# Keeping the first sequence's spectral mixing on chip, with its filters fetched into both partition halves

## The chip, the cores and the metric

The kernel runs on one core of one Trainium2 chip. The metric is device microseconds (us) of one execution, lower is better. "Fast" below means that a run lies within 1.5% of the fastest of its kernel.

PE is TensorE (matrix products), DVE VectorE, ACT ScalarE, POOL GpSimd, and SP SyncE, which only issues transfers here. The transfers that one of them issues are its queue. A matrix product leaves its result in a bank of PSUM (the `ps` tiles of the kernel); copying it out is an eviction. The granted clock is the share of PE's full clock that it was allowed. An item's lag is how much later its Silu instruction starts than that of the same item in the kernel before.

## The reference, cut to what matters

The lines are merged and shortened; they compute the same.

```python
def _attn_ref(x, filt_r, filt_i):              # x: 8 x 3008 x 256, filters: 1505 x 256
    X = np.fft.rfft(x, axis=1)
    return np.fft.irfft(X * (filt_r + 1j * filt_i)[None], n=x.shape[1], axis=1)

def _moe_ref(x, w_gate, w_val, w_out, rms_g):  # 24064 tokens, d_model 256, d_ff 1536
    xn = x / np.sqrt(np.mean(x * x, axis=-1, keepdims=True) + 1e-06) * rms_g
    g = xn @ w_gate
    return (g / (1.0 + np.exp(-g)) * (xn @ w_val)) @ w_out
```

Each of the 8 sequences is mixed along time by a filter in the frequency domain ("mixing"). Every token then passes through a normalization and a gated feed-forward network (FFN).

## The kernel before

The transform of length 3008 = 47 x 64 is made of matrix multiplications. Step A transforms over 64, B over 47, then comes the product with the filters, then B and A backward. Between A and B, and between the two backward steps, the data must change their layout. The kernel does that by writing to DRAM and reading back: `z` between A and B, `g` behind B backward.

The FFN is 8 x 6 x 12 = 576 items of the same work. Mixing of sequence b+1 runs between the items of sequence b, so it is mostly hidden. Mixing of sequence 0 has nothing to hide behind: it is **the opening**, the time before the first gate matmul (`pg`).

The filters are fetched by POOL's queue, chunk by chunk (8 of the 32 frequency columns each), into the lower half of the partitions, in transfers of 24, 16 and 7 rows. On-chip copies make the upper half, with the sign of the imaginary filter turned:

```python
def f_load(c):
    for src, dst in ((filt_r, fr), (filt_i, fi)):
        t = dst[c]
        nc.gpsimd.dma_start(t[0:24, :, :].rearrange("p a d -> p (a d)"),
                            raw(src, c * KC, [[64 * D, 24], [1, KC * D]]))
        lo = 1 if c == 0 else 0
        for a, e in ((0, 16), (16, 23)):
            nc.gpsimd.dma_start(t[32 + a:32 + e, lo:KC, :],
                                raw(src, 64 * (a + 1) - c * KC - lo,
                                    [[64 * D, e - a], [-D, KC - lo], [1, D]]))
        ...
def f_dup(c):
    nc.vector.tensor_copy(out=fr[c][HALF:P], in_=fr[c][0:HALF])
    nc.scalar.activation(out=fi[c][HALF:P], in_=fi[c][0:HALF], func=AXT.Copy, scale=-1.0)
...                                   # the opening, cut
for c in range(NC):
    for i in range(3):
        a_unit(0, 3 * c + i)          # A
    z_store(0, c)                     # to DRAM
for c in range(3):
    t2_load(0, c)                     # and back
gate(st[0]["t2"][0][0:1, 0, 0:1])     # POOL waits for the first reload ...
f_load(1); f_load(2)                  # ... before it issues more filters
f_dup(0)
for i in range(19):
    if i < 16:
        b_unit(0, i)                  # B and the products with the filters (DVE, POOL)
    ...                               # f_load(3), f_dup(1..3), FFN weights
    if i >= 3:
        bi_unit(0, i - 3)             # B backward
        if i % 2 == 0:
            g_store(0, i // 2 - 2)    # to DRAM
for c in range(NXC):
    t4_load(0, c)                     # and back
norm_first()                          # A backward, normalization
```

Of the kernel before, what the change touches and what calls it, by code (L numbers as in the profile page):

```python
# [10 lines left out]
FP32 = mybir.dt.float32  # L11
# [24 lines left out]
KC = 8  # L36


def _make_tables():
# [21 lines left out]
    for k2 in range(K2):  # L61
        for s in range(48):

            if s < 24:
                k = k2 + 64 * s
                sign, q = 1.0, s
            else:
                j = s - 23
                k = 64 * j - (k2 if k2 else 32)
                sign, q = -1.0, 32 + s - 24  # L70
                if j == 24 and k2:
                    continue
# [25 lines left out]
    wi0 = wi[:, 0] * S_INV_B  # L98
    return wa.astype(f), (wai * S_INV_A).astype(f), wb.astype(f), wi0.astype(f), np.eye(P).astype(f)
# [3 lines left out]
def kernel(  # L103
# [13 lines left out]
    wa_np, wai_np, wb_np, wi0_np, id_np = _make_tables()  # L117
    wa_d = nc.inline_tensor(wa_np, name="wa_t").ap()
    wai_d = nc.inline_tensor(wai_np, name="wai_t").ap()
    wb_d = nc.inline_tensor(wb_np, name="wb_t").ap()  # L120
    wi0_d = nc.inline_tensor(wi0_np, name="wi0_t").ap()
    id_d = nc.inline_tensor(id_np, name="id_t").ap()
# [8 lines left out]
    t1p = ctx.enter_context(tc.tile_pool(name="t1p", bufs=2))  # L131
    t2p = ctx.enter_context(tc.tile_pool(name="t2p", bufs=3))
    sp = ctx.enter_context(tc.tile_pool(name="sp", bufs=3))
    ssp = ctx.enter_context(tc.tile_pool(name="ssp", bufs=3))
# [4 lines left out]
    rp = ctx.enter_context(tc.tile_pool(name="rp", bufs=2))  # L139
# [3 lines left out]
    op = ctx.enter_context(tc.tile_pool(name="op", bufs=2))  # L143
# [7 lines left out]
    wai = glob.tile([P, P], FP16)  # L151
    ident = glob.tile([P, P], FP16)
    wb = glob.tile([KR, K2, P], FP16)
    wi = glob.tile([P, K2, 2, P], FP16)
    fr = [glob.tile([P, KC, D], FP32, name="fr%d" % c) for c in range(K2 // KC)]
    fi = [glob.tile([P, KC, D], FP32, name="fi%d" % c) for c in range(K2 // KC)]
# [24 lines left out]
    def bank(i, name):  # L181

        pool, tag = ((psM, "mx"), (psG, "pg"), (psV, "pv"), (psB, "mb"))[i]
        return pool.tile([P, 512], FP32, tag=tag, name=name)

    def a_unit(b, i):
        c, r = divmod(i, XC // 2)
        if r == 0:

            st[b]["t1"][c] = (t1p.tile([P, XC, D], FP16, tag="t1", name="t1") if b else  # L190
                              t4p.tile([P, XC, D], FP16, tag="t4", name="t1"))
        ps = bank(0 if b else i % 3, "psa")
        dst = st[b]["t1"][c][:, 2 * r:2 * r + 2, :]
        nc.tensor.matmul(ps, wa, st[b]["x"][c][:, 2 * r:2 * r + 2, :], start=True, stop=True)  # L194
        src = ps.rearrange("p (a d) -> p a d", a=2)
        nc.scalar.activation(out=dst, in_=src, func=AXT.Copy)  # L196
# [13 lines left out]

    def b_unit(b, i):
        ps = bank(3 if b else (0, 1, 3)[i % 3], "psb").rearrange("p (a d) -> p a d", a=2)
        for u in range(2):
            k = 2 * i + u
            nc.tensor.matmul(ps[:, u, :], wb[:, k, :], st[b]["t2"][k // KC][:, k % KC, :],  # L215
                             start=True, stop=True)
        c, r = divmod(2 * i, KC)
        f1, f2 = fr[c][:, r:r + 2, :], fi[c][:, r:r + 2, :]
        if b:
            s1 = sp.tile([P, 2, D], FP16, tag="s1", name="s1")  # L220
            s2 = sp.tile([P, 2, D], FP16, tag="s2", name="s2")
# [8 lines left out]
        if (b == 0 and i % 2 and i > 4) or (b == 1 and i % 3 == 1):  # L230
            eng = nc.gpsimd
            v = yp.tile([P, 2, 512], FP32, tag="y", name="v")
            v = v[:, 0, :].rearrange("p (a d) -> p a d", a=2)
            nc.scalar.activation(out=v, in_=ps, func=AXT.Copy)
            ps = v
# [3 lines left out]

    def swap_unit(b, i, h):  # L240
# [3 lines left out]
        if h:  # L244
            s = ssp.tile([P, 2, D], FP16, tag="s", name="s")
# [3 lines left out]
    def bi_unit(b, i):  # L249
        ss = st[b]["s"].pop(i)  # L250
        ps = bank(0 if b else 2, "psi").rearrange("p (a d) -> p a d", a=2)
        n = len(ss)
        for u in range(2):
            for q in range(n):
                nc.tensor.matmul(ps[:, u, :], wi[:, 2 * i + u, q, :], ss[q][:, u, :],  # L255
# [10 lines left out]
    def t4_load(b, c):  # L266
        t = t4p.tile([P, XC, D], FP16, tag="t4", name="t4")
        w = XC - 1 if c == NXC - 1 else XC
        for h in range(2):
            for ri in range(2):  # L270
# [3 lines left out]
                (nc.scalar if b == 0 and c == 0 and h else nc.sync).dma_start(  # L274
                    t[p0:p0 + 32, 0:wh, :], g_d[b, :, r0:r0 + wh, :])
# [7 lines left out]
    def n_unit(b, m, dh):  # L283
# [5 lines left out]
        for q in range(nq(b, m)):  # L289
            n1p = 4 * m + q  # L290
            nc.tensor.matmul(ps[:, ts(q, P)],  # L291
                             st[b]["t4"][n1p // XC][:, n1p % XC, ds(dh * P, P)], wai,
# [32 lines left out]
    def rho_load(b, m):  # L325
        rb = rp.tile([P, 4 * P], FP32, tag="rb", name="rb")
# [4 lines left out]
    def norm_first():  # L331
# [3 lines left out]
        for dh in range(2):  # L335
            ps = bank(1 + dh, "psn")
            for q in range(4):
                nc.tensor.matmul(ps[:, ts(q, P)], st[0]["t4"][q // XC][:, q % XC, ds(dh * P, P)], wai,
# [6 lines left out]
        q_unit(0, 0)  # L345
        scale_split(0)
        scale_apply(0, 1)
# [35 lines left out]
    po_of = {}  # L383

# [15 lines left out]
    def down(b, m, jt):  # L400
# [11 lines left out]
        if jt == JT - 1:  # L412
            o3 = op.tile([P, 4, D], FP32, tag="o3", name="o3")
# [22 lines left out]
    def f_load(c):  # L436
        for src, dst in ((filt_r, fr), (filt_i, fi)):
            t = dst[c]
            nc.gpsimd.dma_start(t[0:24, :, :].rearrange("p a d -> p (a d)"),
                                raw(src, c * KC, [[64 * D, 24], [1, KC * D]]))  # L440
            lo = 1 if c == 0 else 0
            for a, e in ((0, 16), (16, 23)):
                nc.gpsimd.dma_start(t[32 + a:32 + e, lo:KC, :],
                                    raw(src, 64 * (a + 1) - c * KC - lo,
                                        [[64 * D, e - a], [-D, KC - lo], [1, D]]))
            if c == 0:
                nc.gpsimd.dma_start(t[32:56, 0, :], raw(src, 32, [[64 * D, 24], [1, D]]))

    def f_dup(c):
        nc.vector.tensor_copy(out=fr[c][HALF:P], in_=fr[c][0:HALF])  # L450
        nc.scalar.activation(out=fi[c][HALF:P], in_=fi[c][0:HALF], func=AXT.Copy, scale=-1.0)

    def wi_group(g):

        ps = bank(1 + g % 2, "pst").rearrange("p (a d) -> p a d", a=4)
        lo = 1 if g == 0 else 0
        for a in range(lo, 4):
            nc.tensor.matmul(ps[:, a, :], wb[:, 4 * g + a, :], ident[0:KR, :], start=True, stop=True)
        k = slice(4 * g + lo, 4 * g + 4)
        nc.scalar.activation(out=wi[:, k, 0, :], in_=ps[:, lo:4, :], func=AXT.Copy, scale=S_INV_B)  # L460
        for p0 in (0, HALF):
            nc.vector.tensor_scalar(out=wi[p0:p0 + HALF, k, 1, :],
                                    in0=ps[HALF - p0:P - p0, lo:4, :], scalar1=S_INV_B,
                                    scalar2=None, op0=ALU.mult)
# [13 lines left out]
    def wb_load(c):  # L478
        nc.sync.dma_start(wb[:, c * KC:(c + 1) * KC, :], wb_d[:, c * KC:(c + 1) * KC, :])

    with tc.manual_schedule():
# [5 lines left out]
        nc.sync.dma_start(wa, wa_d)  # L487
        nc.sync.dma_start(ident, id_d)
        wb_load(0)
        wb_load(1)  # L490

        for c in range(NC):
            for t in (fr[c], fi[c]):
                if c < 2 or (c == 2 and t is fr[c]):
                    nc.vector.memset(t[0:HALF], 0.0)
                else:
                    nc.scalar.activation(out=t[0:HALF].rearrange("p a d -> p (a d)"),
                                         in_=mhalf[0:HALF, 0:1].to_broadcast([HALF, KC * D]),
                                         func=AXT.Copy, scale=0.0)
        nc.vector.memset(ones, 1.0)  # L500
        f_load(0)
        for c in range(NC):
            for i in range(3):
                a_unit(0, 3 * c + i)
            z_store(0, c)
            if c == 1:
                wb_load(2)
                wb_load(3)
                wi_group(0)
                wi_group(1)  # L510
        for c in range(3):
            t2_load(0, c)
        gate(st[0]["t2"][0][0:1, 0, 0:1])
        f_load(1)
        f_load(2)
        nc.sync.dma_start(wi[:, 0], wi0_d)
        nc.sync.dma_start(wai, wai_d)
        with nc.allow_non_contiguous_dma(reason="one gain a partition"):
            nc.sync.dma_start(gsb, moe_rms_g.rearrange("(a p) -> p a", p=P))
        for g in range(2, 8):  # L520
            wi_group(g)
        f_dup(0)
        for i in range(19):
            if i < 16:
                b_unit(0, i)
            if i == 5:
                t2_load(0, 3)
                f_load(3)
            if i == 9:
                w_load(0)  # L530
            if i % 4 == 2 and i // 4 + 1 < NC:
                f_dup(i // 4 + 1)
            if i >= 3:
                bi_unit(0, i - 3)
                if i % 2 == 0:
                    g_store(0, i // 2 - 2)
        for c in range(NXC):
            t4_load(0, c)
        gate(st[0]["t4"][0][0:1, 0, 0:1])
        norm_first()  # L540
        w_load(1)
        w_load(2)
        for dh in range(2):
            n_unit(0, 1, dh)
            sq_unit(0, 1, dh)
        for c in range(NXC):
# [25 lines left out]
        for b in range(1, B):  # L572
# [19 lines left out]
            for i in range(16):  # L592
# [5 lines left out]
                at(s0 + lag, bi_unit, b, i)  # L598
                if i % 2 == 1:
# [54 lines left out]
```

## Time and profile before

The median is 968.98 us of 3 runs (965.85 to 969.09). The profiled execution has a span of 965.5 us.

| what | value | view |
|---|---|---|
| TensorE (PE) busy from 300 to 900 us | 596.87 of 600 us, clock 1.00 | table of stretches |
| first gate matmul | 84.48 us | timeline |
| z round trip: last eight stores issued, first B matmul | 18.9 to 22.5, 28.41 us | timeline |
| g round trip: last eviction, end of reload | 71.09, 76.20 us | chain of waits |

The page cuts the span into 40 slices of 24 us. Each digit is a busy share, or the granted clock, in tenths.

```profile
PE   3345978898999999999999999999999999999997
PEclk8566999999999999999999999999999999999999
DMA  8869774764357345753457535742354322422211
```

PE is starved in the first four slices and nearly full from the eleventh on. Only the opening has much to give. The next lines are from the table of stretches of the kernel before. The columns are the stretch, its length, busy time and instruction count of PE, PE weight loads, DVE, ACT and POOL, then the granted clock, the mean busy share of the 16 DMA engines, and GB/s.

```profile
15.00:20.00 5.00, 0.54 (x7) 0.24 (x4) 2.86 (x5) 1.94 (x4) 0.00 (x0) 0.61 0.93 261
35.00:41.00 6.00, 0.93 (x5) 0.48 (x4) 3.06 (x4) 0.00 (x0) 2.91 (x4) 0.50 0.82 108
300.00:900.00 600.00, 596.87 (x4187) 375.12 (x4185) 458.10 (x722) 420.31 (x717) 237.81 (x178) 1.00 0.46 103
```

From 15 to 20 us (mostly tables and z) the DMA engines moved 261 GB/s at share 0.93. From 35 to 41 us (filters alone) they moved 108 GB/s at share 0.82.

This is the chain of waits of the kernel before (start, duration, what):

```profile
28.43 0.61 POOL gate L469
...
30.66 8.87 DMA fi<-in_filt_i_dram
...
39.81 6.26 DMA fi<-in_filt_i_dram
...
50.57 6.67 DMA fi<-in_filt_i_dram
...
71.11 2.27 DMA g_tmp<-t
...
73.58 2.63 DMA t<-g_tmp
```

Two round trips stand in the chain (`gate` waits for the z reload, then `g_tmp`), and three waits for filters lie between them.

### The profile page before, as it was taken

To read this page: it belongs to the slowest core of one execution; us is meant where nothing else is said; L and a number is where in the kernel's file an instruction comes from. 1 tells how busy PE (TensorE), PEld (TensorE's weight loads), DVE (VectorE), ACT (ScalarE), POOL (GpSimd) and SP (SyncE) were. 2 spreads that over 40 slices of the span, in tenths; PEclk is the share of its full clock that TensorE was granted. 3 is DMA by queue.
4 is the path that set the end of the run, shared out by engine and by line. 5 is a ranking of instruction groups with operands and counts; after the bars stand their busy time and mean duration, and the time that the engine had idled before them with its cause. 6 is when DMAs were issued, how large, how long until landed. Compare 5 with 4: busy or idle time off the path is not lost.

```text
span 965.5 us, 17242 instructions
## 1 busy us (share of the span) xinstructions
PE 880.0 (91%) x6031; PEld 547.8 (57%) x6031; DVE 668.1 (69%) x1039; ACT 630.1 (65%) x1066; POOL 373.1 (39%) x325
## 2 busy tenths in 40 slices
PE   3345978898999999999999999999999999999997
PEld 1223545565655666666666666566666666666654
DVE  6633445577777788687877878688868888555554
ACT  7343667576766776577766776587756776576543
POOL 3474335325551455226542445135522554033200
PEclk8566999999999999999999999999999999999999
DMA  8869774764357345753457535742354322422211
GB/s 196 141 119 174 158 166 108 149 165 91 87 110 171 81 87 110 162 137 95 94 119 159 114 89 90 171 101 72 100 116 112 89 61 58 117 62 53 47 34 44
DMA packets 95542, 106.45 MB, mean 110 GB/s; under 512 B 17304, under 2 KB 70680, under 8 KB 95264
## 3 DMA queue, kind: packets, MB, share of 16 engines
q1 hardware_dynamic: 85808, 87.39, 38.1%
q0 software_dynamic: 9552, 17.77, 12.1%
q8 instruction: 47, 0.77, 0.3%
q14 instruction: 39, 0.32, 0.1%
q10 hardware_dynamic: 96, 0.20, 0.1%
HBM read 70.09 MB, written 49.90 MB: 124 GB/s over the span
## 4 chain that ended last, share of the span: by engine, by line
PE 70%; DMA 10%; issue 6%; DVE 6%; POOL 4%; ACT 3%; SPq 1%; POOLq 0%; DVEq 0%; ACTq 0%
PE po L409 21%; PE pg L392 21%; PE pv L392 20%; DVE hh L397 3%; PE psi L255 3%; DMA fi<-in_filt_i_dram 2%; DMA rb<-r_tmp 2%; PE psb L215 2%; PE psn L291 2%; PE psa L194 2%; DVE o L415 1%; DMA t<-g_tmp 1%; POOL s L246 1%; DMA z_tmp<-t 1%; DMA g_tmp<-t 1%
## 5 line engine op out<-in xcount | busy, mean ns | idle before, releaser
L397 DVE TENSOR_TENSOR hh<-pv,sg 128x512 f16<-128x512 f32 (+1 forms) x576 | 391.6, 680 | 231.4 <-ACT sg L396 114.3
L396 ACT ACTIVATE sg<-pg 128x512 f16<-128x512 f32 (+1 forms) x576 | 338.8, 588 | 241.6 <-PE pg L392 232.7
L409 PE MATMUL po<-wo,hh 128*128 128x256 f16 x2256 | 343.2, 272 | 2.7 <-DVE o L415 1.3
L392 PE MATMUL pg<-xn,wg 128*128 128x512 f16 (+1 forms) x1152 | 338.4, 375 | 0.0
L392 PE MATMUL pv<-xn,wv 128*128 128x512 f16 (+1 forms) x1152 | 338.3, 375 | 0.0
L409 PEld LDWEIGHTS <-hh 128*128 128x128 f16 x2256 | 216.2, 98 | 112.7 <-issue 13.1
L246 POOL TENSOR_TENSOR s<-s,s 128x512 f16<-128x512 f16 x96 | 110.6, 1152 | 359.9 <-DVE s L243 290.4
L392 PEld LDWEIGHTS <-wv 128*128 128x128 f16 x1152 | 112.7, 98 | 131.6 <-issue 1.1
L377 POOL TENSOR_TENSOR xn<-y,rb 128x1024 f16<-128x1024 f32 (+1 forms) x46 | 128.8, 2800 | 59.2 <-DMA rb<-r_tmp 52.1
L243 DVE TENSOR_TENSOR s<-psb,fi 64x512 f16<-64x512 f32 x192 | 132.1, 688 | 5.9
L392 PEld LDWEIGHTS <-wg 128*128 128x128 f16 x1152 | 109.1, 98 | 13.8 <-issue 1.8
L260 ACT ACTIVATE t<-psi 96x512 f16<-96x512 f32 x128 | 75.4, 592 | 29.0 <-PE psi L255 16.5
L296 ACT ACTIVATE y<-psn,gsb 128x512 f32<-128x512 f32 (+1 forms) x94 | 63.7, 678 | 12.5 <-PE psn L291 4.8
L317 POOL TENSOR_TENSOR rho<-u,mhalf 128x4 f32<-128x4 f32 (+1 forms) x48 | 48.4, 1009 | 56.5 <-DVE u L315 56.1
L255 PEld LDWEIGHTS <-wi 128*128 128x128 f16 x320 | 32.6, 103 | 65.1 <-issue 29.0
L223 DVE TENSOR_TENSOR s<-psb,fr 128x512 f16<-128x512 f32 x96 | 65.5, 682 | 4.7 <-PE psb L215 4.2
L196 ACT ACTIVATE t<-psa 128x512 f16<-128x512 f32 x96 | 56.4, 602 | 12.6 <-PE psa L194 6.6
L215 PE MATMUL psb<-t,wb 96*128 96x256 f16 x256 | 51.6, 286 | 9.4 <-DMA t<-z_tmp 8.8
L255 PE MATMUL psi<-s,wi 128*128 128x256 f16 x256 | 46.2, 272 | 9.9 <-POOL s L246 5.7
L302 ACT ACTIVATE sq<-psn 128x512 f16<-128x512 f32 (+1 forms) x94 | 54.8, 582 | 0.0
L194 PE MATMUL psa<-xc,wa 128*128 128x512 f16 x96 | 36.9, 398 | 16.7 <-DMA xc<-in_x_dram 9.2
L291 PEld LDWEIGHTS <-t 128*128 128x128 f16 x368 | 28.7, 99 | 21.9 <-issue 1.2
(58 smaller groups left out, 382.4 us busy)
## 6 DMA issues: line engine op xcount, KB each, us to landing
out_dram<-o SPq DMA_DIRECT2D x84, 256.0 KB, 3.3
z_tmp<-t SPq DMA_DIRECT2D x128, 96.0 KB, 2.4
t<-z_tmp SPq DMA_DIRECT2D x32, 384.0 KB, 5.1
g_tmp<-t SPq DMA_DIRECT2D x64, 192.0 KB, 3.4
xc<-in_x_dram POOLq DMA_DIRECT2D x56, 192.0 KB, 6.0
rb<-r_tmp SPq DMA_DIRECT2D x42, 256.0 KB, 4.4
t<-g_tmp SPq DMA_DIRECT2D x102, 96.0 KB, 3.1
out_dram<-o SPq DMA_DIRECT2D x12, 192.0 KB, 3.0
```

Of the source, the lines that this page charges most:

```text
L215: nc.tensor.matmul(ps[:, u, :], wb[:, k, :], st[b]["t2"][k // KC][:, k % KC, :], start=True, stop=True)
L223: nc.vector.tensor_tensor(out=s1, in0=ps, in1=f1, op=ALU.mult)
L243: nc.vector.tensor_tensor(out=s2[a], in0=ps[e], in1=f2[e], op=ALU.mult)
L246: nc.gpsimd.tensor_tensor(out=s, in0=s1, in1=s2, op=ALU.add)
L255: nc.tensor.matmul(ps[:, u, :], wi[:, 2 * i + u, q, :], ss[q][:, u, :], start=(q == 0), stop=(q == n - 1))
L260: nc.scalar.activation(out=st[b]["t3"][c][:, 2 * r:2 * r + 2, :], in_=ps[0:KR], func=AXT.Copy)
L296: nc.scalar.activation(out=y[:, dh, 0:w], in_=ps[:, 0:w], func=AXT.Identity, scale=gsb[:, dh:dh + 1])
L377: nc.gpsimd.tensor_tensor(out=xv, in0=yv, in1=rv.unsqueeze(1).to_broadcast([P, 2, n, P]), op=ALU.mult)
L392: nc.tensor.matmul(ps[:, 0:w], wt[:, dt_, ts(jt, P)], xn[:, dt_, 0:w], start=(dt_ == 0), stop=(dt_ == 1))
L396: nc.scalar.activation(out=sg[:, 0:w], in_=pg[:, 0:w], func=AXT.Silu)
L397: nc.vector.tensor_tensor(out=hh[:, 0:w], in0=pv[:, 0:w], in1=sg[:, 0:w], op=ALU.mult)
L409: nc.tensor.matmul(po[s4 // 2][:, s4 % 2, :], hh[:, ts(s4, P)], wo[:, jt, :], start=(jt == 0 and s4 % 2 == 0), stop=(jt == JT - 1 and (s4 ...
```

## The change

Its intent: sequence 0 no longer goes through DRAM. A and B backward are computed with operands swapped, so that channels lie on the partitions, and 16-bit transposes on PE change the layout. Filters are fetched straight into both halves of the partitions (chunk 0 is still copied), so no copies are needed. The imaginary filter arrives with the same sign in both halves; sequence 0 is served by a table `ws` with turned signs. Sequences 2 and later need the sign in the upper half, and four POOL passes (`negate`) turn it while sequence 1 is mixed.

```diff
-    def f_load(c):
+    def f_load(c, p0, part):
+        n, k0 = FC[c], (0, 8, 16)[c]                  # chunks of 8, 8 and 16 columns
...
+            if part == 0:
+                nc.sync.dma_start(t[p0:p0 + 24, :, :].rearrange("p a d -> p (a d)"),
+                                  raw(src, k0, [[64 * D, 24], [1, n * D]]))
...
+            a, e = ((0, 16), (16, 23))[part - 1]
+            eng = nc.gpsimd if (part == 2 and c) else nc.sync
+            eng.dma_start(t[p0 + 24 + a:p0 + 24 + e, lo:n, :],
+                          raw(src, 64 * (a + 1) - k0 - lo, [[64 * D, e - a], [-D, n - lo], [1, D]]))
...
+    def negate(c, r, n):
+        t = fi[c][HALF:P, r:r + n, :]
+        nc.gpsimd.tensor_scalar(out=t, in0=t, scalar1=-1.0, scalar2=None, op0=ALU.mult)
+    def at_unit(m, dh): ...      # A: x is the stationary operand, channels on partitions
+    def t1_unit(g): ...          # 8 transposes with a strided source, 1 or 2 evictions
+    def bit_unit(i): ...         # B backward: 8 matmuls of 96 columns per unit
+    def t2_unit(j, eng): ...     # 4 transposes, one eviction
...
-            z_store(0, c)
-            t2_load(0, c)
-                    g_store(0, i // 2 - 2)
-            t4_load(0, c)
+        for part in range(3):
+            for p0 in (0, HALF):
+                f_load(1, p0, part)
...                               # chunk 2 likewise
+        for i in range(16 + LAG):
+            if i < 16:
+                b_unit(0, i)
+            if i % 2 == 0 and i // 2 + 2 < 8:
+                t1_unit(i // 2 + 2)
+            if i >= LAG:
+                bit_unit(i - LAG)
...
+                if b == 1 and i in (3, 7, 11, 15):
+                    at(s0 + 2, negate, min(i // 4, 2), 8 if i == 15 else 0, 8)
```

## The prediction

The 200 GB/s stands as an estimate, between the measured 108 (filters alone) and 261 GB/s (tables and z). The sum: 3.9 of some 9 MB by 20 us, the rest at 200 GB/s gives the last filters at 42 to 46 us, eight DVE units of 1.38 us from 42 us on end at 53 to 54, and with 13 us behind them the first gate matmul comes near 66 us, 18 us earlier. The 13 us, and the "1 or 2 us" for sign flips and reload, are estimates too. The "cold" 0.13 us was measured at a granted clock of 0.50 (the kernel before, 77 to 78 us).

> **What bounds the kernel now.** The table of stretches shows two regimes. Between 300 and 900 us TensorE is the limit (99% busy, clock 1.00). Up to 85 us it starves: mostly below half busy, at granted clock 0.5 for much of the time after 15 us. The timeline puts the first gate matmul at 84.4 us. Nearly all of the change's worth is how much earlier that matmul starts.
>
> The chain of waits in the opening is made of transfers: x until about 14 us; the z store and reload (last store issued at 18.9, first B matmul at 28.4 us); then filters, issued one behind another by POOL (waits of 8.9, 6.3 and 6.7 us on fi), with halves copied by DVE and ACT (1.2 to 2.1 us each); then g store and reload (70.5 to 77.0 us). From the first normalization matmul to the first gate matmul are 7.4 us.
>
> **Removed.** z round trip: about 10 us. g round trip: about 6.5 us. Three of four pairs of filter copies, most weight-table copies on DVE, POOL's serial issue of filters.
>
> **Added.** 112 transposes, and 128 narrow matmuls instead of 64 wide ones. Cold 128x128 pairs of load and matmul take about 0.13 us (8 in 1.03 us at 77 us), so 112 transposes are about 15 us of TensorE time, mostly hidden behind filter transfers. All final transposed tiles are queued before the first gate matmul: I estimate 13 us from the last mixing eviction to that matmul, where 7.4 us were needed after the reload. Filters for both halves raise their bytes from 3.1 to about 5.4 MB. Four POOL sign flips and a reload of the B table fall into sequence 1; 1 or 2 us at most.
>
> **The new limit** should be the filter transfers. Filters alone moved 108 GB/s at DMA share 0.82 (35 to 41 us); tables and z moved 261 GB/s at 0.93 (15 to 20 us). [...] I take 200 GB/s: some 9 MB (x, tables, filters, first FFN weights), 3.9 MB of it moved by 20 us as before, gives the last filters at 42 to 46 us; I use 42. Eight B units remain, each DVE unit 1.38 us: mixing ends near 54 us, first gate matmul near 66 us, 18 us earlier. FFN weights are also issued earlier; waiting for them cost about 2 us near 93 us before.
>
> **Predicted: 948 us, 936 to 961 in 8 of 10 cases.** Chances: faster by over 2% 0.55, within 2% 0.42, slower 0.03.
>
> **What would show it.** Timeline: first gate matmul at 58 to 75 us. DMA view: no z or g round trip in sequence 0, filters at 180 GB/s or more. Chain of waits: transfers into the third filter chunk, then DVE products, then transposes. From the first gate matmul to the end: 0 to 3 us shorter.
>
> **What would make it wrong.** Filters still near 110 GB/s (last landing after 52 us): then 955 to 965 us. Transposes reading columns at a stride of 48 or 64 bytes far slower than 0.13 us, lengthening the tail after mixing. Sign flips on POOL delaying sequence 1. Or a shorter tail and faster transfers: 935 us.

## The result

The changed kernel is correct. Its median is 981.14 us (979.2 to 982.72, 4 runs) against 969.04 us (965.85 to 969.21, 4 runs) of the kernel before on the same chip. The ratio is 1.0132, with a 95% interval of 1.0101 to 1.0163. Ratios here are the mean time of one kernel's fast runs over that of the other's in the same rounds, so not quite the ratio of the quoted medians. The change made the kernel 1.3% slower, where 2% faster was expected.

The page of the kernel after:

```profile
PE   5517978888899999999999999999999999999997
PEclk7757999999999999999999999999999999999999
DMA  9988574575247544575357445653345323422211
```

PE works more in the first two slices and then almost stops in the third (49 to 74 us). The first gate matmul, from the timelines of before and then after, shows how much later the FFN starts:

```profile
84.48 1.06 PE L392 MATMUL pg<-xn,wg 128*128 128x512 f16 x2
```

```profile
90.93 1.06 PE L407 MATMUL pg<-xn,wg 128*128 128x512 f16 x2
```

It is 6.45 us later instead of 18 us earlier. The table of stretches of the kernel after says what was going on:

```profile
25.00:35.00 10.00, 8.04 (x87) 7.12 (x86) 6.66 (x10) 6.61 (x10) 2.52 (x2) 0.66 0.89 124
35.00:45.00 10.00, 1.41 (x18) 1.04 (x15) 2.48 (x4) 2.23 (x4) 3.27 (x3) 0.77 1.00 127
45.00:55.00 10.00, 3.81 (x47) 3.46 (x46) 0.00 (x0) 3.14 (x6) 3.91 (x5) 0.67 1.00 119
55.00:65.00 10.00, 0.00 (x0) 0.00 (x0) 0.00 (x0) 0.00 (x0) 0.00 (x0) 0.50 1.11 157
```

For ten microseconds no engine computes anything, and the DMA engines are busy all the time (the share adds up the packets' recorded times over the 16 engines, so at 1.11 records overlap). From 25 to 55 us they move 119 to 127 GB/s, not far from the poor rate of the filters before (108), while the bytes to fetch have grown. In the empty stretch they move 157 GB/s, and 0.6 of these 1.6 MB are the first FFN weights, on POOL's queue (by the packet records). The chain of waits of the kernel after is one row of transfers:

```profile
10.24 14.02 DMA fr<-in_filt_r_dram
24.28 15.39 DMA fr<-in_filt_r_dram
39.69 19.34 DMA fi<-in_filt_i_dram
59.04 9.77 DMA gsb<-in_moe_rms_g_dram
...
76.33 1.65 ACT gT L516 x4
...
90.12 1.01 PE pt L527 x8
```

And DVE's timeline shows when the products could go on (the bracket is the idle time before, and what ended it):

```profile
41.71 0.69 DVE L249 TENSOR_TENSOR sg<-psb,fr 128x512 f16<-128x512 f32 x1 [9.24 <-DMA fr<-in_filt_r_dram]
...
67.22 0.69 DVE L249 TENSOR_TENSOR sg<-psb,fr 128x512 f16<-128x512 f32 x1 [23.04 <-DMA fr<-in_filt_r_dram]
68.85 0.69 DVE L250 TENSOR_TENSOR hh<-psb,fi 128x512 f16<-128x512 f32 x1 [0.94 <-DMA gsb<-in_moe_rms_g_dram]
```

Line 250 reads `fi`. The label `gsb`, a transfer of 1 KB that landed in the same instant, is only the last one by the profile. What the line needs is the last part of `fi`, of the same queue. So the last filters were usable at 67 to 69 us, where the prediction had 42.

The second loss is behind the first gate matmul. Comparing the starts of the 576 Silu instructions item by item with the kernel before, the kernel after is 4.95 us late at item 8 and 15.5 us late at the last item. That is a loss of 10.5 us between these two items. From the first gate matmul to the end of the span, the kernel after needs 889.9 us and the kernel before 881.0: 9 us were lost, where 0 to 3 us of gain were predicted.

### The profile page after: what moved, and what is told of

Its sections match the earlier page's. It is cut to its first block, busy times and chain, and to the rows that moved or that the text cites. A ratio compares the mean times of both kernels' runs of the same rounds, so it can differ in the third digit from the quotient of the medians.

```text
span 980.9 us, 17647 instructions
## 1 busy us (share of the span) xinstructions
PE 895.9 (91%) x6253; PEld 564.8 (58%) x6253; DVE 661.0 (67%) x1041; ACT 625.1 (64%) x1064; POOL 385.3 (39%) x310
## 4 chain that ended last, share of the span: by engine, by line
PE 72%; DMA 11%; DVE 5%; POOL 4%; issue 4%; ACT 2%; SPq 1%; POOLq 0%; DVEq 0%; ACTq 0%
PE po L424 21%; PE pg L407 21%; PE pv L407 20%; DMA fr<-in_filt_r_dram 3%; DVE hh L412 3%; PE psi L272 3%; PE psb L229 2%; DMA fi<-in_filt_i_dram 2%; PE psn L307 2%; DMA rb<-r_tmp 2%; PE psa L199 1%; DVE o L430 1%; DVE s L260 1%; DMA z_tmp<-t 1%; POOL s L263 1%
## 5 line engine op out<-in xcount | busy, mean ns | idle before, releaser
L277 ACT ACTIVATE t<-psi 96x512 f16<-96x512 f32 x112 | 66.3, 592 | 24.0 <-PE psi L272 19.2
L201 ACT ACTIVATE t<-psa 128x512 f16<-128x512 f32 x84 | 50.1, 597 | 11.5 <-PE psa L199 5.9
L272 PEld LDWEIGHTS <-wi 128*128 128x128 f16 x256 | 25.0, 98 | 42.3 <-issue 17.1
L229 PE MATMUL psb<-t,wb 96*128 96x256 f16 x224 | 43.6, 276 | 5.8 <-DMA t<-z_tmp 5.8
L199 PE MATMUL psa<-xc,wa 128*128 128x512 f16 x84 | 31.8, 379 | 7.0 <-ACT t L277 3.2
```

The lines of the kernel that those rows point to most:

```text
L229: nc.tensor.matmul(ps[:, u, :], (wb if b else wbp)[:, k, :], st[b]["t2"][k // KC][:, k % KC, :], start=True, stop=True)
L272: nc.tensor.matmul(ps[:, u, :], wi[:, q, 2 * i + u, :], ss[q][:, u, :], start=(q == 0), stop=(q == n - 1))
L277: nc.scalar.activation(out=st[b]["t3"][c][:, 2 * r:2 * r + 2, :], in_=ps[0:KR], func=AXT.Copy)
```

## The experiments

Theory A: the filters' transfers are slow because each writes few neighbouring partitions, and the change nearly doubled those bytes (3.1 to 5.4 MB). Rivals: the pitch of the source rows (64 KB) slows them in DRAM (B); the added bytes alone are to blame (C). For the second loss: the four sign passes on POOL (D), or clock drops of PE that vary from run to run (E).

### e1: without the sign passes

```diff
-                if b == 1 and i in (3, 7, 11, 15):
-                    at(s0 + 2, negate, min(i // 4, 2), 8 if i == 15 else 0, 8)
```

The result is wrong (sequences 2 and later).

> The changed kernel without the four sign flips on POOL (wrong result on purpose from sequence 2 on). If the flips (5.4 us of POOL each, behind which products and normalizations of sequence 1 queue) are the loss after the first gate matmul, the lag of this kernel behind the kernel before stays at 4 to 6 us from the tenth FFN tile to the end instead of growing to 15.5 us, and the time is 9 to 12 us below the changed kernel: about 970 us. If the rest of the change (reload of the B table, other placement in memory) causes that loss, the lag still grows and the time stays above 977 us.

Measured: 980.37 us (975.58 to 981.82, 4 runs), ratio to before 1.0116 [1.0081, 1.0151]. That is within noise of the kernel after (1.0132). The lag of the stream grew by 5.7 us from item 8 to the end instead of 10.5, but in the profiled run the opening was 5 us longer (first gate matmul at 95.88 us), so the times of this pair settle nothing. The 5.7 us that stay without the passes show that they are not the whole of the second loss.

### e2: filters into one half, copied on chip

```diff
-            for p0 in (0, HALF):
-                f_load(1, p0, part)
+            f_load(1, 0, part)                       # chunk 2 likewise
...
+            if i in (4, 8, 12):                      # copies the lower half of 8 columns up
+                f_dup(min(i // 4, 2), 8 if i == 12 else 0)
```

Correct result.

> The changed kernel with filters fetched into the lower half only, and copied to the upper half by DVE and ACT as in the kernel before (right result). If filter bytes at some 120 GB/s set the end of the mixing, 2.3 MB fewer bytes bring the last filters at about 48 us instead of 67, the first gate matmul at 72 to 76 us instead of 91, and the time to 962 to 968 us (flips still in). If the rival holds, that both halves are nearly free [...] and something else holds the transfers up, the last filters land after 60 us and the time stays above 974 us.

Measured: 964.26 us (960.59 to 967.28, 4 runs), ratio 0.9964 [0.9931, 0.9998]. The first gate matmul came at 78.26 us, 12.7 us earlier than in the kernel after (72 to 76 were expected). DVE's timeline shows the last wait for filters:

```profile
49.77 1.22 DVE L469 COPY fr<-fr 64x2048 f32<-64x2048 f32 x1 [7.74 <-DMA fr<-in_filt_r_dram]
```

So fetching the second half was far from free. But the transfers still ran at 115 and 123 GB/s (25 to 35 and 35 to 45 us), and the filters still bounded the opening. C is a part of the cause, not the whole.

### e3: same bytes, destination rows spread over the partitions

```diff
-                nc.sync.dma_start(t[p0:p0 + 24, :, :]
+                nc.sync.dma_start((t[p0 // HALF:p0 // HALF + 93:4, :, :] if c else t[p0:p0 + 24, :, :])
...                                                   # same rows, 4 partitions apart
-            eng.dma_start(t[p0 + 24 + a:p0 + 24 + e, lo:n, :],
+            q0 = p0 + part + 1
+            eng.dma_start(t[q0:q0 + 4 * (e - a) - 3:4, lo:n, :] if c else t[p0 + 24 + a:p0 + 24 + e, lo:n, :],
```

The filters of chunks 1 and 2 lie in wrong rows, so the result is wrong. Sources, sizes, row counts, queues and order are those of the kernel after.

### e4: same bytes, source rows 61 KB apart

```diff
-                                  raw(src, k0, [[64 * D, 24], [1, n * D]]))
+                                  raw(src, k0, [[(61 if c else 64) * D, 24], [1, n * D]]))
...                                                   # and likewise in parts 1 and 2
```

Its output is wrong, which doesn't matter for the time.

> Same source rows, same sizes, same order of transfers as the changed kernel, but the second and third chunk of the filters land on every fourth partition instead of 24, 16 or 7 neighbouring ones (wrong result on purpose). If the partitions written set the rate, packets of 1 to 16 KB get clearly shorter than now (1 KB: 0.13 us, 16 KB: 1.9 us) and the last filters land before 50 us. If the source (rows 64 KB apart in memory) or the queue sets it, they land at 64 to 70 us as in the changed kernel.

> Same destinations and sizes as the changed kernel, but the rows of one transfer are 61 KB apart in memory instead of 64 KB (wrong result on purpose). If the distance of 64 KB in memory sets the rate, the last filters land before 50 us and packets get shorter; if the partitions written set it, they land at 64 to 70 us as in the changed kernel.

Measured, one look each (state unknown): e3 958.08 us, e4 982.36 us. These are the stretches of e3, then of e4:

```profile
25.00:35.00 10.00, 8.52 (x80) 7.38 (x80) 7.46 (x12) 6.54 (x10) 4.09 (x4) 0.58 0.92 241
35.00:45.00 10.00, 4.44 (x70) 3.77 (x69) 1.73 (x3) 5.67 (x12) 5.70 (x6) 0.94 1.02 218
```

```profile
25.00:35.00 10.00, 7.52 (x69) 6.37 (x68) 6.66 (x10) 6.16 (x9) 2.50 (x2) 0.58 0.91 128
35.00:45.00 10.00, 2.53 (x24) 1.98 (x21) 2.36 (x4) 2.58 (x5) 2.33 (x2) 0.67 0.97 118
```

At about the same DMA share (0.9 to 1.0), e3 moved 241 and 218 GB/s where the kernel after moved 124 and 127. Only the rows written differ. The packet records agree: from 17 to 50 us, packets of 8 KB of SP's queue took 938 ns on average in the kernel after and 474 ns in e3, packets of 16 KB 2122 and 1003 ns. The last filters were usable at 46.3 us, and the first gate matmul came at 68.4 us. In e4, with another source pitch, nothing of this kind happened: the rates were 128 and 118 GB/s, the packets took 856 and 2412 ns, and the first gate matmul came at 93.1 us. **The destination rows set the rate** (241 GB/s for rows 4 apart against 124 for neighbouring ones, 25 to 35 us). Rival B has fallen.

Why neighbouring rows are slower is not shown. For comparison, the filters alone moved 108 GB/s in the kernel before, and stretches of the kernel after moved 113 to 127 GB/s (35 to 41, 35 to 45 us), tables among them. The row counts are no rival, as e3 has those of the kernel after; how many DMA engines share a transfer no view here counts.

### e5: one half, sign turned in the copy, no sign passes

```diff
-    ws = np.concatenate([wf[HALF:P], -wf[0:HALF]], 0)
+    ws = np.concatenate([wf[HALF:P], wf[0:HALF]], 0)
...
-        nc.scalar.activation(out=fi[c][HALF:P, r:r + 8], in_=fi[c][0:HALF, r:r + 8], func=AXT.Copy)
+        nc.scalar.activation(out=fi[c][HALF:P, r:r + 8], in_=fi[c][0:HALF, r:r + 8], func=AXT.Copy,
+                             scale=-1.0)
...                                                   # the negate lines are gone
```

This is e2 without the passes, and correct.

> The one-half kernel, with the sign put into the copy of fi so that the four flips on POOL go (right result). The opening should be as in the one-half kernel (first gate matmul at 78 to 80 us). If the flips cost what they seemed to cost in the changed kernel, 4 to 6 us go in sequence 1 and the time is 958 to 961 us; if they cost nothing, it stays at 963 to 966 us.

Measured: 961.40 us (960.33 to 965.81, 4 runs), ratio 0.9933 [0.9895, 0.9971]. It is some 3 us faster than e2, with intervals that overlap, and on another chip. The sign is in the right direction for D, but D is not shown by this pair.

### e6 and e7: real filters into one half, imaginary ones into the other, at once

e6 fetches `fr` by SP's queue into the lower and `fi` by POOL's queue into the upper half, and copies across (e5's bytes, no sign passes; the second table and one subtraction take over the signs). e7 also interleaves the two kinds of rows, so that a transfer writes every second partition:

```diff
+    def rows_of(t, p0, s0, s1):
+        return t[p0 + s0:p0 + s1]                                         # e6
+        q0 = p0 + (2 * s0 if s0 < 24 else 2 * (s0 - 24) + 1)              # e7
+        return t[q0:q0 + 2 * (s1 - s0) - 1:2]
+    def fr_load(c):
+        f_load(c, nc.sync, filt_r, fr[c], 0)
+    def fi_load(c):
+        f_load(c, nc.gpsimd, filt_i, fi[c], HALF)
+    def f_dup(c=0, r=0):
+        nc.vector.tensor_copy(out=fr[c][HALF:P, r:r + 8], in_=fr[c][0:HALF, r:r + 8])
+        nc.scalar.activation(out=fi[c][0:HALF, r:r + 8], in_=fi[c][HALF:P, r:r + 8], func=AXT.Copy,
+                             scale=-1.0)
```

For e7, the frequency rows of the tables are permuted in the same way (`q = 2 * s` and `q = 2 * (s - 24) + 1`). Both are correct.

> fr goes to partitions 0 to 47 through the SP queue, fi to partitions 64 to 111 through the POOL queue at the same time, and each is copied across; no flips (right result). Same bytes as the one-half kernel, twice as many partition groups written at once. If the partitions written set the rate, the last filters land at 33 to 42 us instead of 51, the first gate matmul is at 62 to 70 us, and the time is 945 to 953 us. If not, the last filters land at 47 us or later and the time is that of the one-half kernel without flips.

> As the split kernel, but the 24 rows of a transfer go to every second partition (0, 2 .. 46; the reversed ones to 1, 3 .. 45), with the columns of the tables permuted to match (right result). If neighbouring partitions share what limits the rate, the last filters land 3 to 8 us earlier than in the split kernel; the mixing itself then limits, and the time is 942 to 950 us. Otherwise the same as the split kernel.

Measured: e6 951.29 us (950.21 to 955.36, 4 runs), ratio 0.9828 [0.9791, 0.9865]. e7 **942.89 us** (941.53 to 944.03, 4 runs), ratio **0.9733 [0.9702, 0.9764]**. These are the last waits for filters: in e5 on ACT, which copies `fi`, then in e6 on DVE, then in e7 on DVE with the first gate matmul:

```profile
52.93 1.91 ACT L470 ACTIVATE fi<-fi 64x2048 f32<-64x2048 f32 x1 [8.57 <-DMA fi<-in_filt_i_dram]
```

```profile
45.91 1.22 DVE L473 COPY fr<-fr 64x2048 f32<-64x2048 f32 x1 [4.79 <-DMA fr<-in_filt_r_dram]
```

```profile
35.47 1.32 DVE L474 COPY fr<-fr 64x2048 f32<-64x2048 f32 x1 [2.24 <-DMA fr<-in_filt_r_dram]
60.83 1.06 PE L407 MATMUL pg<-xn,wg 128*128 128x512 f16 x2
```

The last filters went from 52.9 us (e5) to 45.9 and 35.5 us, with the same bytes. The first gate matmul went from 80.00 to 71.6 and 60.83 us. One stretch of e5, e6 and e7 shows the rate behind it, at nearly the same DMA share:

```profile
15.00:25.00 10.00, 5.72 (x48) 5.00 (x49) 3.69 (x6) 2.80 (x6) 0.00 (x0) 0.50 1.03 89
```

```profile
15.00:25.00 10.00, 7.32 (x70) 6.29 (x68) 5.88 (x9) 5.05 (x8) 2.36 (x5) 0.69 1.08 151
```

```profile
15.00:25.00 10.00, 5.62 (x75) 4.83 (x73) 7.96 (x13) 6.82 (x11) 2.33 (x4) 0.95 1.04 204
```

Writing two halves at once from two queues helps (89 to 151 GB/s), though less than expected (last filters at 33 to 42 us, first gate matmul at 62 to 70), and so does spreading the rows within a half (151 to 204 GB/s). e7 is correct and beats both kernels.

Against e5 of the same rounds, e6's step paid (ratio 0.9828 against 0.9933). e6 differs from e5 in the queues too, so the share of the halves alone is not measured.

### e8: e7 with half of the last transposes moved behind the first gate matmul

```diff
-        for j in range(6, 12):
-            t2_unit(j, j % 2)
...
+        for j in range(6, 12):
+            at(j // 2, t2_unit, j, j % 2, True)      # through the PSUM bank "mx", among the FFN items
+        at(6, setup_end)                             # the rest of the opening's end, too
```

> As the interleaved kernel, and the last six transposed tiles of sequence 0 are made behind the first FFN tiles instead of before the first gate matmul (right result). Six tiles took about 2.8 us before it: 2 to 3 us less than the interleaved kernel if this tail was on the chain, 0 if the first gate matmul waited for something else, such as the weights.

Measured: 947.57 us (944.63 to 949.01, 4 runs), ratio 0.9772 [0.9733, 0.9811], slower than e7 though it was meant to be faster. The first gate matmul came 3.1 us earlier (57.76 us), but at item 8 the stream was already 3.3 us behind e7's, and at the end 5 us behind. The transposes went through a single PSUM bank, and three times PE waited there for the eviction of the one before (2.1 us in all). Work moved behind the start of the FFN was not hidden there.

### e9 and e7 again: the sign passes put back into e7

The four passes stand at their old places, multiplying by 1.0, so the result stays correct:

```diff
-        nc.gpsimd.tensor_scalar(out=t, in0=t, scalar1=-1.0, scalar2=None, op0=ALU.mult)
+        nc.gpsimd.tensor_scalar(out=t, in0=t, scalar1=1.0, scalar2=None, op0=ALU.mult)
...
+                if b == 1 and i in (3, 7, 11, 15):
+                    at(s0 + 2, negate, min(i // 4, 2), 8 if i == 15 else 0, 8)
```

> The interleaved split (e7, median 942.9 us) with the four POOL passes over the B weights put back at their old places, multiplying by 1.0, so the result stays right. Theory A, the passes (5.4 us each, POOL's products and normalized tiles queue behind them) cost the first FFN items time that TensorE does not get back: 4 to 6 us slower than e7 in the same rounds, 946 to 949 us, with the lag of the stream behind the kernel before growing by 8 to 10 us from item 8 to the end, where e7's grew by 3.4 us. Rival B, the larger growth seen with the passes was the run-to-run change of clock drops: within 2 us of e7.

> The interleaved split again, for pairing with the run that puts the four passes back: both theories expect 941 to 945 us.

Measured: e9 949.44 us (944.7 to 950.76, 6 runs), e7 again 945.95 us (943.97 to 947.37, 4 runs). (e7 again is on another chip than e7, and 3 us above it.) The ratio of the means is 0.9797 / 0.9770 = 1.0028, or 2.7 us, between the two expectations; from the scatter of these runs I work out a 95% interval of about 0 to 5.5 us. The lag of the stream grew by 6.4 us from item 8 to the end, with 3.3 us in e7 again. Two more pairs differ in the same direction, none clear of noise by itself: after and e1 by 1.6 us, e2 and e5 by 3 us (ratios times the time before). The traces agree: from item 8 to the end the lag grew by 6.4 to 10.5 us in the five profiled kernels on chip that have the passes (after, e2, e3, e4, e9), and by 2.6 to 5.7 us in the six that do not (e1, e5, e6, e7, e7 again, e8). Here is how the first pass reaches PE: POOL's timeline of e9, then of e7 again.

```profile
122.18 5.39 POOL L255 TENSOR_SCALAR fi<-fi 64x2048 f32<-64x2048 f32 x1
127.65 1.27 POOL L249 TENSOR_TENSOR s<-v,fr 128x512 f16<-128x512 f32 x1
128.88 1.26 POOL L250 TENSOR_TENSOR s<-v,fi 128x512 f16<-128x512 f32 x1
```

```profile
124.56 1.27 POOL L249 TENSOR_TENSOR s<-v,fr 128x512 f16<-128x512 f32 x1 [2.51 <-ACT v L247]
125.79 1.27 POOL L250 TENSOR_TENSOR s<-v,fi 128x512 f16<-128x512 f32 x1
```

One pass takes 5.39 us. The products stand behind it and start 3.1 us later, and PE's timeline of e9 shows it waiting for both:

```profile
128.97 0.27 PE L272 MATMUL psi<-s,wi 128*128 128x256 f16 x1 [0.76 <-POOL s L249]
130.19 0.57 PE L272 MATMUL psi<-s,wi 128*128 128x256 f16 x3 [0.95 <-POOL s L250]
```

Right after the second wait the clock was granted at half for 3.4 us (from 130.5 us), and between items 32 and 36 the stream of e9 fell 3.7 us further behind. e7 again was at half clock just as long in all (6.8 us, from 105.5 us on), so the clock does not make the difference of 3.1 us between the two lags; PE's idle gaps from item 8 on do, with 25.9 us in e9 and 23.4 in e7 again. So POOL's passes are very likely not free, but they are worth some 2 to 3 us, not the whole of the second loss.

### e10: the kernel before, with only its filters fetched as in e7

```diff
-        for src, dst in ((filt_r, fr), (filt_i, fi)):
-            t = dst[c]
-            nc.gpsimd.dma_start(t[0:24, :, :].rearrange("p a d -> p (a d)"),
+        pair = ((filt_r, fr[c], 0), (filt_i, fi[c], HALF))
+        for src, t, p0 in pair:
+            nc.gpsimd.dma_start(t[p0:p0 + 47:2].rearrange("p a d -> p (a d)"),
...                                                   # z and g round trips stay, rows interleaved
```

Correct result.

> The kernel before, z and g round trips kept, but with each chunk's real filters loaded into the lower and its imaginary filters into the upper half of the partitions, rows of the two kinds interleaved, and copied across on chip. Theory A, the on-chip mixing is worth its two round trips (10 and 6.5 us, less about 8 us of longer tail) once the filters no longer hold it back: 950 to 958 us, so 8 to 15 us behind e7. Rival B, the whole gain of e7 is the filters' layout: 941 to 946 us. Rival C, the round trips are what bounds the kernel before and its filters wait for nothing: within 4 us of the kernel before, 964 to 968 us.

Measured: 961.51 us (959.66 to 965.43, 6 runs), ratio 0.9937 [0.9913, 0.9961]. The first gate matmul came at 76.26 us, 8.2 us earlier than before. The round trips stay in its chain of waits:

```profile
63.04 2.25 DMA g_tmp<-t
65.49 2.48 DMA t<-g_tmp
```

Against e7 again of the same rounds the ratio is 0.9937 / 0.9770 = 1.0171, or 16 us, and the first gate matmuls are 76.26 - 61.74 = 14.5 us apart. That is just beyond the 8 to 15 us expected, and the time itself is above the 950 to 958 us of theory A. Neither "it is all the filters' layout" nor "the filters wait for nothing" holds: the layout alone gains 6 us, and the changes that come with mixing on chip (no round trips, filters issued at the start and not behind POOL's gate) are worth 16 us **once the filters come fast enough**.

## Why the prediction was wrong

- **What bounds the kernel** was right: the opening, by transfers; its round trips are worth much, as e10 against e7 shows.
- **The step that failed** is the term "I take 200 GB/s ... gives the last filters at 42 to 46 us; I use 42". From 20 us to the last filters (68.8 us) the DMA engines moved 6.4 MB at 132 GB/s, and the filters were usable at 67 to 69 us. At 200 GB/s the same bytes would have been there at 52 us: the rate is some 17 us of the error. The rest is that 3.3 and not 3.9 MB had been moved by 20 us, that 9.8 and not 9 MB were needed, and that the lower end of the range was used. With 25 to 27 us more in this term the sum gives 91 to 93 us, and the first gate matmul came at 90.93 us. The rest of the sum held: 24 us were predicted from the last filters to the first gate matmul, and 22 to 24 were measured. Of the 33 us between the predicted and the measured time, some 24.5 us are this, and the others lie behind the first gate matmul (below).
- **How it came about**: the prediction assumed that fetching both halves would not cost twice the time of one. No trace showed it, and what a few neighbouring rows cost in either half was not asked. The number that warns of this was in the text itself: filters alone at 108 GB/s with DMA engines 0.82 busy. It was read as agreeing with a cheap second half, when it was the price of the same transfers that the change then nearly doubled. Fetching the second half cost 12.7 us of the first gate matmul (e2).
- **Transposes** were sized right. Eight took 1.01 us (0.13 us each, predicted 0.13) at half clock, strided sources included. From the last mixing eviction (end 77.98 us) to the first gate matmul took 13 us, as predicted.
- **From the first gate matmul to the end**, 0 to 3 us of gain were predicted and 9 us were lost. Up to item 8 the lag fell by 1.3 us (6.25 to 4.95). That is right in sign, and PE's wait of 1.65 us near 93 us in the kernel before, which its chain puts behind a transfer of weights, is gone. From item 8 to the end 10.5 us were lost. The sign passes, "1 or 2 us at most", take 5.4 us each on POOL and cost 1.6 to 3 us in each of three pairs. (A pass has one input and 64 x 2048 32-bit elements: 2.6 ns for an element of a partition, no better than POOL's product of two inputs with 2.5 ns, 512 elements in 1.27 us. DVE copied the same shape in 1.22 us in e2.) Three stretches of half clock (3.4 us each, from 136.0, 159.9 and 248.7 us, none in the profiled kernel before) are an estimate of 3 x 1.7 = 5 us: at clock 0.50 a pair of gate matmuls took 0.85 us until the next matmul, at 1.00 it took 0.43 (before, from 84.48 and 88.03 us), so half of such a stretch is lost. Two of them follow waits of 2.0 and 2.2 us, the third two waits for POOL's products of 0.7 and 0.95 us. PE's idle gaps (over 0.15 us each) from item 8 on sum to 28.3 us against 23.7 before: 4.6 us more, mostly waits for POOL's products and for the reload of `z` (5.8 us against 3.3). Gaps and half clock together make 9.7 of the 10.5 us. The passes can act through both, so their 1.6 to 3 us are not a third term.
- **What stays open**: even without the passes, the stream of every variant with mixing on chip lost 2.6 to 5.7 us against that of the kernel before from item 8 on (e1, e5, e6, e7 and e8; e10, without mixing on chip, lost 0.9 us). The same sum, the change of the gaps plus half of the time at half clock, comes within about 1 us of the loss in all eleven other profiles (e7: -0.8 + 3.4 for 2.6 us; e5: -0.5 + 5.1 for 4.9 us). So what stays is mostly half clock, of which the one profile of the kernel before has none there. What brings the extra half clock about is open: the new order of POOL's work and the reload of the B table in sequence 1 are candidates, and no run separates them. The length of the wait does not decide it alone here: in e9, waits of 0.76 and 0.95 us within 2 us were followed by half clock, and in the kernel after, a wait of 3.55 us (from 199.1 us) was followed by no drop (granted clock 1.00 from 196 to 206 us).
- **"What would make it wrong"** named the right cause first (filters still near 110 GB/s) but priced it at 955 to 965 us. That can have counted neither the added bytes at that rate nor the loss in the stream.

## What to carry to other kernels

Before moving work from one resource to another, price the load on the resource that is left: a change that removes two round trips lost because it nearly doubled transfers that already ran at 108 GB/s where others moved 261. When DMA engines are busy and GB/s are low (share 1.03 at 89 GB/s in e5, 1.04 at 204 in e7), look at the partitions that are written: here, spreading rows over the partitions and writing two halves from two queues took the same bytes from 52.9 to 35.5 us. And test a rejected idea again once its real limit is gone: with the filters' layout changed, mixing on chip was worth 16 us.
